# Attention and feed-forward on one core: exponents of the first block read from PSUM in pieces of 64 columns, one pair of banks for all quads, and a new order

## The chip, the cores and the metric

The kernel runs on one core of a Trainium2 chip. The metric is the device time of one execution in microseconds (us); less is better. TensorE multiplies, VectorE (DVE) and ScalarE (ACT) do the elementwise work, and SyncE (SP) issues the DMAs. Each engine works through its own queue in order; a queue's head that waits holds back all that stands behind it.

## What is computed

Chunked attention (32 queries against 8 memory keys, 16 keys to the left, the 32 of the chunk and 8 to the right, so 64 keys), then a feed-forward of two matrices with a squared, clipped activation between them:

```python
for c in range(24):                                   # chunks of 32 of a sequence of 768; batch 4, heads 8, head_dim 64
    scores = scale * q_c @ k_full.T                   # 32 x 64
    scores = scores - max(scores)                     # of each row
    a = exp(scores); a = a / (sum(a) + 1e-9)
    out[c] = a @ v_full
x = out as 3072 tokens x 512
h = x @ w_in                                          # 512 x 2048
g = where(h >= 1, h, where(h <= -1, 0, (h + 1)**2 / 4))
result = g @ w_out                                    # 2048 x 512, float32
```

## The kernel before

The tokens are cut into six blocks of 512. Blocks 0 and 1 go through the feed-forward with plain products, in steps of 128 columns of the hidden layer: `half_step` for half a block (A and B in the order), `step` for a whole one (E and F). Each float32 operand is split into a high and a low float32r part, and three products stand for one. Blocks 2 to 5 use a seven-product scheme: `product` makes the first layer by quads of four hidden slices (four quads per block), `unit` the second layer. The weights arrive by 16 loads of 1 MB as 64-bit words, which `decode` (w) turns into the two parts; `build` (t) and `build_out` (T) later make the sums that the seven products need.

`first_attention(g)` (g0 to g3) is the attention of block 0 in four units; units 0 and 1 are the first half of the block's tokens, 2 and 3 the second. For one unit: TensorE makes scores in PSUM (128 rows x 512 columns, that is 8 groups of 64), VectorE takes the maximum of each group (`mx`) and writes scores less maximum to SBUF (`pr`), ScalarE takes one exponent over the 512 columns, VectorE sums (`den`), adds 1e-9, inverts (`rin`) and multiplies; TensorE transposes `pr` into a bank, ScalarE copies it (`pt`), TensorE multiplies it with the values (`ps_x`), and ScalarE and VectorE split the result into `xth` and `xtl`. Units 2 and 3 keep their scores in the same pair of banks (`a1`, in `PLACES`). The loads of the four units' `first_qk` stand among the weights on the one DMA queue (`LOADS`). Nothing of the feed-forward can start before units 0 and 1 are through.

What stands where on each engine is written out by hand: `ORDER` is a table of some 1,860 names, each of which advances one piece of work by one step, and each engine keeps that order. `begin_second` (B in the table) takes the two `ps_h` banks for the quads as X and Y. In block 2, `bank_of` gives the second quad (n == 1) two other banks, `ps_g`, out of the four that the sums `ps_o` of blocks 0 and 1 have freed. A quad's result is read from X and Y by copies, relus and additions (`copy_out`, `relus`, `add_up`).

All instructions are issued through one helper, so every row names L150; rows are told apart by their tiles.

Of the kernel before, what the change touches and what calls it, by code (L numbers as in the profile page):

```python
# [9 lines left out]
F32 = mybir.dt.float32  # L10
# [18 lines left out]
    + + + + + g0 g0 g0 + g0 g1 + g1 g0 g0 g1 w0 g1 g0 g0 g1 g0 + + g1 g1 g1 w0 g2 g1 g0 g0 g1 g1 +  # L29
    g2 g2 w0 g2 g0 w0 g1 g2 g2 g3 + + g2 g2 w1 g2 + g0 g1 w0 + g3 g3 g3 w1 g3 g3 A0 g3 w2 g3 g2 A0  # L30
    g3 w1 A0 g2 w0 g3 w1 + g2 + w0 g3 g2 g3 + g3 A1 w3 w1 w1 B0 A2 + A1 w2 B0 w2 + w1 A0 A2 B0 A0
    B0 B1 A1 A0 w5 A2 w3 w3 B2 B0 w2 A1 A1 w4 w2 w3 w5 B1 B2 + + w3 B0 w4 w5 A1 + w6 B1 A3 A2 B3 B1
    A2 w4 A2 + n0 + B1 A3 A3 E4 B2 w5 w5 B2 B3 w4 B2 w7 B3 n0 A3 n0 w6 E4 w9 E6 w4 A3 n0 w8 E5 w7
    w6 B3 B3 E5 w7 w7 E4 B1 w6 w10 A3 E5 w7 w9 B3 E4 E8 E4 E5 E6 E5 w6 n0 w12 E4 B2 E6 + E8 w8 w9
    E6 w8 w9 + E7 w8 E6 E7 E5 w11 E8 E4 w9 E7 w11 w14 n0 w11 E6 E8 w8 w11 w11 E5 E8 w10 E7 E10 n0
    E9 E10 E7 w10 w10 w14 n0 E10 n0 w10 E8 E7 w14 + E9 E7 w12 E8 w14 E11 w13 w12 E9 n0 w12 E9 E10
    E10 E12 E9 E12 w15 w12 E9 n0 E6 n0 E11 w13 E12 E9 E11 n0 w14 w15 w13 n0 E11 E12 E13 E11 w13 w15
    E10 E13 w13 E13 n0 E12 n0 E14 n0 E12 E14 E11 n1 t1 n0 E10 t1 E14 C0 E12 n1 w15 E14 + E13 n1 E13
    E11 n1 n1 C0 n1 n1 n1 C1 + n1 E14 C1 n1 n1 w15 C2 E15 C0 n1 n1 E15 E13 E15 n1 E13 E15 n1 C0 t1
    E15 n1 n1 t1 n1 C2 C1 E15 E14 t1 D0 C2 E15 E14 C2 E15 C1 D0 E15 D1 C1 C0 C3 n2 E15 F4 E15 C0 D1  # L40
# [1112 lines left out]
```

## Time and profile before

| | |
|---|---|
| median of 3 runs | 576.08 us (574.78 to 576.36) |
| the profiled execution's own time | 575.56 us |
| its span, first to last instruction | 573.7 us |
| TensorE busy | 557.2 us (97%) |
| VectorE busy | 473.8 us (83%) |
| ScalarE busy | 368.0 us (64%) |
| mean granted TensorE clock | 0.988 of full speed |

The span is the time from the first to the last instruction; 1.9 us of the profiled execution lie outside it. Busy times are of instructions, which overlap a little at their ends on VectorE and ScalarE. A wait is named by what came last before it ended.

### The profile page before, as it was taken

Reading aid. Unit: us, or ns where it says so; the run is one execution under the profiler, and the core shown is the slowest. Engines: PE = TensorE matmul, PEld = TensorE weight load, DVE = VectorE, ACT = ScalarE, POOL = GpSimd, SP = SyncE. Lnnn points to the kernel's source line nnn. Section 1 sums busy time; section 2 is a strip of 40 time slices with the busy share of each in tenths; the row PEclk is TensorE's granted clock in tenths of the full one; section 3 lists DMA queues with packets and bytes.
Section 4 is the critical chain, followed back from the end, with each engine's and each line's share of the span. In section 5 each row is a group of like instructions: output and inputs, shape, how many; then the busy total and the mean of one; then the engine's idle time right before and its main releaser. Section 6 shows DMA issues by size and latency. Waiting matters only on the chain.

```text
span 573.7 us, 15814 instructions
## 1 busy us (share of the span) xinstructions
PE 557.2 (97%) x6648; PEld 516.1 (90%) x6648; DVE 473.8 (83%) x870; ACT 368.0 (64%) x677; POOL 0.7 (0%) x6
## 2 busy tenths in 40 slices
PE   5799999999999999999999999999999999999997
PEld 3798888888888889899999999999999999999997
DVE  5899996866998988999999769888867979566696
ACT  2699967564656684696766656756576576565642
POOL 0000000000000000000000000000000000000000
PEclk8699999999999999999999999999999999999999
DMA  8999600505798757789978979888869956789432
GB/s 348 422 422 418 282 0 2 184 7 198 272 359 324 270 197 251 266 271 354 327 267 273 322 229 349 289 309 286 269 203 316 328 197 209 238 238 309 153 111 92
DMA packets 40758, 145.72 MB, mean 254 GB/s; under 512 B 4208, under 2 KB 4464, under 8 KB 36080
## 3 DMA queue, kind: packets, MB, share of 16 engines
q1 hardware_dynamic: 40688, 144.72, 71.6%
q8 instruction: 52, 0.85, 0.6%
q14 instruction: 18, 0.15, 0.1%
HBM read 115.34 MB, written 29.36 MB: 252 GB/s over the span
## 4 chain that ended last, share of the span: by engine, by line
PE 88%; DMA 6%; DVE 3%; ACT 2%; issue 1%; DVEq 0%
PE ps_o L150 41%; PE ps_h L150 41%; PE ps_x L150 3%; DMA qk<-in_first_qk_dram 3%; PE ps_s L150 3%; DMA wr<-saved 2%; DMA out_dram<-ob 1%; DVE pr L150 1%; PE ps_g L150 1%; DVE feo L150 1%; ACT gw L150 0%; DVE ob L150 0%; ACT gt L150 0%; DVE wr L150 0%; DVE f L150 0%
## 5 line engine op out<-in xcount | busy, mean ns | idle before, releaser
L150 PE MATMUL ps_h<-s,wr 128*128 128x256 f32 x720 | 94.4, 282 | 0.3 <-DMA wr<-saved 0.2
L150 PEld LDWEIGHTS ps_h<-s,wr 128*128 128x128 f32 x720 | 89.1, 188 | 0.9 <-DVE gsb L150 0.4
L150 PE MATMUL ps_h<-xth,wr 128*128 128x512 f32 (+1 forms) x320 | 89.0, 354 | 0.2 <-ACT wr L150 0.2
L150 PE MATMUL ps_o<-wr,gh 128*128 128x512 f32 x256 | 80.6, 396 | 0.0
L150 PE MATMUL ps_h<-a,wr 128*128 128x256 f32 x540 | 70.9, 282 | 0.4 <-issue 0.3
L150 PEld LDWEIGHTS ps_h<-a,wr 128*128 128x128 f32 x540 | 67.4, 188 | 0.9 <-issue 0.4
L150 PEld LDWEIGHTS ps_h<-xth,wr 128*128 128x128 f32 x320 | 57.0, 190 | 9.4 <-ACT wr L150 0.3
L150 PEld LDWEIGHTS ps_o<-wr,gh 128*128 128x128 f32 x256 | 47.2, 188 | 10.4
L150 PE MATMUL ps_h<-xtl,wr 128*128 128x512 f32 (+1 forms) x160 | 54.4, 352 | 0.0
L150 PE MATMUL ps_o<-wr,gsd 128*128 128x256 f32 x384 | 53.8, 282 | 0.0
L150 PE MATMUL ps_o<-wr,gsc 128*128 128x256 f32 x384 | 52.8, 282 | 0.0
L150 PE MATMUL ps_o<-wr,gsb 128*128 128x256 f32 x320 | 50.8, 282 | 0.0
L150 PE MATMUL ps_o<-wr,gl 128*128 128x512 f32 x128 | 50.5, 394 | 0.0
L150 PEld LDWEIGHTS ps_o<-wr,gsd 128*128 128x128 f32 x384 | 49.0, 188 | 0.1
L150 PEld LDWEIGHTS ps_o<-wr,gsc 128*128 128x128 f32 x384 | 48.6, 188 | 0.2 <-DVE gsc L150 0.2
L150 ACT ACTIVATE gw<-ps_h 128x512 f32<-128x512 f32 (+1 forms) x55 | 29.6, 539 | 28.3 <-PE ps_h L150 19.8
L150 PEld LDWEIGHTS ps_o<-wr,gsb 128*128 128x128 f32 x320 | 43.9, 188 | 0.2
L150 ACT ACTIVATE gw<-gw 128x512 f32<-128x512 f32 (+1 forms) x72 | 42.6, 592 | 0.6
L150 ACT COPY gt<-ps_h 128x512 f32<-128x512 f32 x45 | 26.2, 583 | 16.7 <-PE ps_h L150 14.2
L150 PEld LDWEIGHTS ps_h<-xtl,wr 128*128 128x128 f32 x160 | 30.7, 192 | 4.3
L150 DVE TENSOR_TENSOR gt<-gt,ps_h 128x512 f32<-128x512 f32 x30 | 20.4, 680 | 12.0 <-ACT gt L150 5.9
L150 ACT COPY pt<-pr 32x512 f32<-32x512 f32 x40 | 24.7, 618 | 8.2 <-DVE pr L150 7.4
(106 smaller groups left out, 1012.0 us busy)
## 6 DMA issues: line engine op xcount, KB each, us to landing
wr<-saved SPq DMA_DIRECT2D x112, 512.0 KB, 4.9
w<-in_w_dram SPq DMA_DIRECT2D x16, 1024.0 KB, 18.6
qk<-in_qk_dram SPq DMA_DIRECT2D x10, 1536.0 KB, 7.1
v<-in_vw_dram SPq DMA_DIRECT2D x10, 1024.0 KB, 7.3
saved<-st SPq DMA_DIRECT2D x16, 512.0 KB, 4.0
plain_g<-gw SPq DMA_DIRECT2D x32, 256.0 KB, 4.7
gr<-plain_g SPq DMA_DIRECT2D x16, 512.0 KB, 4.4
saved<-wr SPq DMA_DIRECT2D x24, 256.0 KB, 4.0
```

The costliest lines, as they stand in the source:

```text
L150: return self.tc.keep_in_program_order(getattr(self.engine, name)(*args, **kwargs))
```

## The change

Three things change, and no arithmetic is left out.

1. In `first_attention`, for all four units (`BY_ROWS`), VectorE no longer writes scores less maximum and no longer sums. It multiplies the maxima by -scale (8 columns), and ScalarE takes the exponents straight from PSUM in eight activations of 64 columns, each with one column of `mx` as its bias and one column of `den` as its running sum.
2. `bank_of` loses its case for the second quad of block 2, which now uses X and Y like all others.
3. `ORDER` is written anew, with the same names but for one step less in each of g0 to g3. `LOADS`, and so the sequence on the DMA queue up to block 1, is the same.

```diff
 ORDER = """
-    + + + + + g0 g0 g0 + g0 g1 + g1 g0 g0 g1 w0 g1 g0 g0 g1 g0 + + g1 g1 g1 w0 g2 g1 g0 g0 g1 g1 +
...
-    def normalise(pr):
+    def normalise(pr, den=None):
         n = pr.shape[1]
-        den = apool.tile([P, n], F32, name="den", bufs=2)
-        dve.tensor_reduce(den, pr, axis=AX.X, op=ALU.add)
-        yield
+        if den is None:
+            den = apool.tile([P, n], F32, name="den", bufs=2)
+            dve.tensor_reduce(den, pr, axis=AX.X, op=ALU.add)
+            yield
         dve.tensor_scalar_add(den, den, 1e-9)
...
+    BY_ROWS = (0, 1, 2, 3)
...
-        p4 = pr.rearrange("p (h n) w -> p h n w", h=2)
-        dve.tensor_tensor(p4, s, m3.unsqueeze(3).to_broadcast([P, 2, n, W]), op=ALU.subtract)
-        yield
-        act.activation(pr, pr, AF.Exp, scale=SCALE)
-        yield
-        yield from normalise(pr)
+        if g in BY_ROWS:
+            dve.tensor_scalar(mx, mx, -SCALE, None, op0=ALU.mult)
+            yield
+            den = apool.tile([P, NG], F32, name="den", bufs=2)
+            for i in range(NG):
+                h, k = divmod(i, n)
+                act.activation(
+                    pr[:, i], s[:, h, k], AF.Exp, bias=mx[:, i : i + 1], scale=SCALE, accum_out=den[:, i : i + 1]
+                )
+            yield
+            yield from normalise(pr, den)
...
     def bank_of(name, key):
-        n = order[SECOND].index(key[1])
-        if key[0] == SECOND and n == 1:
-            if (n, name) not in bank:
-                for k in range(2):
-                    bank[n, "XY"[k]] = single(2 * n - 2 + k, "ps_g")
-            return bank[n, name]
         return bank[name]
```

**First place: the start of ScalarE's queue.** `pr_145` and `pr_138` hold units 0 and 1, `pr_324` and `pr_336` units 2 and 3; `w_105` and `w_176` are the first weights. Before:

```order
L150 ACT_TABLE_LOAD
L150 ACTIVATE pr_145<-pr_145 128x512 [waits DVE_49]
L150 ACTIVATE w_105<-w_105 128x1024 [waits DMAHW2_49]
L150 ACTIVATE pr_145<-pr_145 128x512 [waits DVE_49]
L150 COPY pt_146<-ps_h 128x512 [waits PE_49] x2
L150 ACTIVATE pr_324<-pr_324 128x512 [waits DVE_49]
```

After:

```order
L150 ACT_TABLE_LOAD [waits DVE_49]
L150 ACTIVATE pr_138,den<-ps_s,mx 128x64 [waits PE_49]
L150 ACTIVATE pr_138,den<-ps_s,mx 128x64 x7
L150 ACTIVATE w_176<-w_176 128x1024 [waits DMAHW2_49]
L150 ACTIVATE pr_138,den<-ps_s,mx 128x64 [waits DVE_49,PE_49]
L150 ACTIVATE pr_138,den<-ps_s,mx 128x64 x7
L150 CAST wr_258<-f 128x2x256 [waits DVE_49,Activation_49]
L150 COPY pt_139<-ps_h 128x512 [waits PE_49] x2
L150 CAST wr_258<-f 128x2x256
L150 ACTIVATE pr_336,den<-ps_s,mx 128x64 [waits DVE_49,Activation_49]
L150 ACTIVATE pr_336,den<-ps_s,mx 128x64 x7
L150 CAST xth<-ps_x 128x2x256 [waits PE_49]
```

Each exponent of 512 columns has become eight rows of 64. The load of the activation table stood free at the head of the queue; it now stands behind a wait for VectorE, whose first result for ScalarE is the scaled maximum of unit 0.

**Second place: VectorE's queue from the end of unit 2 to the end of unit 3.** Before, with `f` and `wr` the pieces of the weights' decoding:

```order
L150 TENSOR_TENSOR xtl<-ps_x,xth 128x2x256 [waits Activation_49] x2
L150 TENSOR_TENSOR wr_334<-f,wr_334 128x2x256
L150 TENSOR_REDUCE mx<-ps_s 128x8 [waits PE_49]
L150 TENSOR_TENSOR pr_324<-ps_s,mx 128x512 [waits DVE_49]
L150 TENSOR_SCALAR f<-w_206 128x1024 [waits DMAHW7_49,Activation_49]
L150 TENSOR_REDUCE den<-pr_324 128x8 [waits Activation_49]
L150 TENSOR_SCALAR den<-den 128x8 [waits DVE_49]
L150 RECIPROCAL rin<-den 128x8 [waits DVE_49]
L150 TENSOR_TENSOR pr_324<-pr_324,rin 128x512 [waits DVE_49]
L150 SCALAR_TENSOR_TENSOR f<-w_206,f 128x1024
```

After:

```order
L150 RECIPROCAL rin<-den 128x8 [waits DVE_49]
L150 TENSOR_TENSOR pr_336<-pr_336,rin 128x512 [waits DVE_49,PE_49]
L150 TENSOR_TENSOR wr_258<-f,wr_258 128x2x256
L150 TENSOR_TENSOR xtl<-ps_x,xth 128x2x256 [waits Activation_49]
L150 TENSOR_SCALAR f<-w_267 128x1024 [waits DMAHW7_49,Activation_49]
L150 TENSOR_REDUCE mx<-ps_s 128x8 [waits PE_49]
L150 TENSOR_SCALAR mx<-mx 128x8 [waits DVE_49]
L150 TENSOR_TENSOR xtl<-ps_x,xth 128x2x256 [waits Activation_49]
L150 SCALAR_TENSOR_TENSOR f<-w_267,f 128x1024
L150 TENSOR_SCALAR den<-den 128x8 [waits Activation_49]
L150 RECIPROCAL rin<-den 128x8 [waits DVE_49]
L150 TENSOR_TENSOR pr_336<-pr_336,rin 128x512 [waits DVE_49]
```

The two wide steps between a unit's maximum and its 1e-9 are gone; the 1e-9 of unit 2 (the row just ahead of the piece) and its multiplication, a low part of the weights, the first `xtl` and a shift of the second weights now stand ahead of the maximum of unit 3, and the other `xtl` and the second weights' long step between its scaled maximum and its 1e-9.

**Third place: ScalarE's queue at the second quad of block 2.** The copy of the quad's third sum is the row `gt<-ps_g` before, and the last row `gt<-ps_h` after. Before:

```order
L150 CAST wr_861<-feo 128x2x256
L150 CAST gsb<-gk 128x512
L150 CAST gsc<-gs 128x512
L150 COPY gt<-ps_g 128x512
L150 CAST wr_945<-feo 128x256
L150 COPY pt<-pr 32x512 x2
```

After:

```order
L150 CAST wr_786<-feo 128x256
L150 COPY ob<-ps_o 128x512
L150 COPY gt<-ps_h 128x512
L150 CAST gsb<-gk 128x512
L150 CAST wr_784<-feo 128x2x256
L150 COPY u_3055<-ps_h 128x512
L150 COPY gt<-ps_h 128x512
L150 CAST gsc<-gs 128x512
```

The cast of `gsc`, which takes a sum of VectorE's, stood ahead of that copy and now stands behind it.

On TensorE there, the third sum's product (`s_2648` before, `s_2680` after) and the next product on the same bank (`a_2651` before):

```order
L150 MATMUL ps_g<-s_2648,wr_1095 128x256 [waits DMAHW6_49,Activation_49]
L150 MATMUL ps_g<-s_2648,wr_1095 128x256 x11
L150 MATMUL ps_h<-a_2511,wr_962 128x256 [waits DMAHW7_49]
L150 MATMUL ps_h<-a_2511,wr_962 128x256 x11
L150 MATMUL ps_g<-a_2651,wr_1052 128x256 [waits DMAHW0_49,Activation_49]
L150 MATMUL ps_g<-a_2651,wr_1052 128x256 x11
L150 MATMUL ps_g<-s_2816,wr_1114 128x256 [waits DMAHW1_49,DVE_49]
```

After:

```order
L150 MATMUL ps_h<-s_2680,wr_1220 128x256 [waits DMAHW4_49,Activation_49]
L150 MATMUL ps_h<-s_2680,wr_1220 128x256 x11
L150 MATMUL ps_o<-wr_445,gsa 128x256 [waits PE_49]
L150 MATMUL ps_o<-wr_445,gsa 128x256
L150 MATMUL ps_o<-wr_445,gsa 128x256 [waits DVE_49]
L150 MATMUL ps_o<-wr_658,gsa 128x256 x3
L150 MATMUL ps_o<-wr_598,gsb 128x256 x2
L150 MATMUL ps_o<-wr_598,gsb 128x256 [waits DVE_49]
L150 MATMUL ps_o<-wr_740,gsb 128x256 x3
L150 MATMUL ps_o<-wr_258,gsb 128x256 [waits PE_49]
L150 MATMUL ps_o<-wr_258,gsb 128x256 x2
L150 MATMUL ps_o<-wr_598,gsb 128x256 x3
```

Before, one product of 12 matmuls for another quad stood between the two. Now 18 matmuls of the second layer (`ps_o`, of `gsa` and `gsb`) do; the next row after the piece is the quad's next product on that bank.

## Rows read from the trace of the kernel before

**Rows 1.** The page's head: span, and TensorE's busy time.

```profile
span 573.7 us, 15814 instructions
...
PE 557.2 (97%) x6648; PEld 516.1 (90%) x6648; DVE 473.8 (83%) x870; ACT 368.0 (64%) x677; POOL 0.7 (0%) x6
```

**Rows 2.** Stretches: length, busy us (and instructions) by engine, granted clock, DMA.

```profile
0.00:10.00 10.00, 5.05 (x136) 2.41 (x136) 3.81 (x9) 2.49 (x3) 0.70 (x6) 1.00 0.79 319
10.00:20.00 10.00, 6.88 (x200) 5.88 (x200) 8.93 (x18) 5.46 (x9) 0.00 (x0) 0.55 1.02 419
20.00:30.00 10.00, 8.33 (x222) 7.79 (x223) 7.42 (x13) 6.27 (x13) 0.00 (x0) 0.77 1.02 424
```

**Rows 3.** TensorE's waits in the whole span: us in total, times, longest.

```profile
PE ps_s L150 <- DMA qk<-in_first_qk_dram: 4.3, 4, 2.3
PE ps_h L150 <- DVE pr L150: 4.2, 2, 3.3
...
PE ps_g L150 <- ACT gt L150: 1.4, 1, 1.4
```

**Rows 4.** TensorE in order of time, units 0 to 3: start, us, operation, [idle before].

```profile
13.75 1.11 PE L150 MATMUL ps_h<-ident,pr 128*128 128x128 f32 x4
14.79 3.64 PE L150 MATMUL ps_x<-pt,v 64*64 64x32 f32 x128
...
20.72 1.29 PE L150 MATMUL ps_s<-qk 64*32 64x64 f32 x64 [2.29 <-DMA qk<-in_first_qk_dram]
...
26.18 0.63 PE L150 MATMUL ps_h<-ident,pr 128*128 128x128 f32 x4 [0.95 <-DVE pr L150]
26.73 2.07 PE L150 MATMUL ps_x<-pt,v 64*64 64x32 f32 x128
```

**Rows 5.** VectorE in order of time: the first maximum, then unit 3.

```profile
6.17 0.69 DVE L150 TENSOR_REDUCE mx<-ps_s 128x8 f32<-128x512 f32 x1
...
22.05 0.69 DVE L150 TENSOR_REDUCE mx<-ps_s 128x8 f32<-128x512 f32 x1 [1.64 <-PE ps_s L150]
...
24.17 0.69 DVE L150 TENSOR_REDUCE den<-pr 128x8 f32<-128x512 f32 x1
24.89 0.17 DVE L150 TENSOR_SCALAR den<-den 128x8 f32<-128x8 f32 x1
...
25.34 0.69 DVE L150 TENSOR_TENSOR pr<-pr,rin 128x512 f32<-128x512 f32 x1
25.95 1.22 DVE L150 SCALAR_TENSOR_TENSOR f<-w,f 128x1024 uint32<-128x1024 uint32 x1
```

**Rows 6.** ScalarE in order of time: its first row, then unit 3 and after.

```profile
0.73 1.28 ACT L150 ACT_TABLE_LOAD   x1 [0.73 <-PEq L1139]
...
23.50 0.64 ACT L150 ACTIVATE pr<-pr 128x512 f32<-128x512 f32 x1 [3.39 <-DVE pr L150]
24.05 1.14 ACT L150 ACTIVATE w<-w 128x1024 f32<-128x1024 f32 x1
25.09 0.56 ACT L150 COPY pt<-ps_h 128x512 f32<-128x512 f32 x1
25.55 0.38 ACT L150 ACTIVATE gw<-ps_h 128x256 f32<-128x256 f32 x1
25.83 0.38 ACT L150 ACTIVATE gt<-ps_h 128x256 f32<-128x256 f32 x1
```

**Rows 7.** ScalarE's activations out of PSUM by shape: busy us, mean ns.

```profile
L150 ACT ACTIVATE gw<-ps_h 128x512 f32<-128x512 f32 x39 | 23.4, 599 | 25.5 <-PE ps_h L150 17.0 <-DVE gl L150 6.1 <-DMA wr<-saved 2.3
...
L150 ACT ACTIVATE gw<-ps_h 128x256 f32<-128x256 f32 x16 | 6.3, 392 | 2.8 <-PE ps_h L150 2.7
```

**Rows 8.** TensorE in order of time at block 2's second quad.

```profile
244.54 1.69 PE L150 MATMUL ps_g<-a,wr 128*128 128x256 f32 x12 [1.41 <-ACT gt L150]
```

**Rows 9.** ScalarE there: the cast and the copy behind it.

```profile
243.24 0.62 ACT L150 CAST gsc<-gs 128x512 fp32r<-128x512 f32 x1 [0.92 <-DVE gs L150]
243.90 0.59 ACT L150 COPY gt<-ps_g 128x512 f32<-128x512 f32 x1
```

More of the change, by code (lines that the diff above doesn't have):

```diff
@@ new lines @@
+    F4 t4 F4 C1 t1 t4 + D2 F6 D3 t2 F5 F7 t4 t2 t4 F6 t2 t4 n2 t4 n2 n2 F6 n2 F6 F6 D2 t2 t2 F5 F5
+    t5 D2 F4 + F8 F5 n2 D2 t5 t5 D3 C3 F5 t2 n2 t5 n2 t5 t2 t2 t5 F5 F8 t5 t3 F8 t5 F8 t7 D3 n2 F9
+    D3 F5 t3 n2 D2 n2 t3 F7 t3 F8 D2 t7 t3 D1 t7 F9 n2 t7 t7 t3 F11 t7 t3 F9 D3 F7 F9 t7 F10 t3 F7
+    t6 t6 F9 F11 F8 t7 t6 t6 t6 F11 T0 n3 F7 F8 F12 n2 T0 F11 T0 T0 t6 T0 n3 T0 F10 F10 F9 F11 t6
+    n3 T0 n3 F10 F13 t6 n3 n3 T1 T1 T1 T1 F11 T1 F10 n3 n2 T0 T1 n3 n3 F10 F13 T0 T1 n3 T1 + n3 F13
@@ new lines @@
+    30c3 2u6r 2u4ld 2u4q3 4x 2u4q6 3kS4 30a22 3jS4 2u5s3 2u5s1 30m11 30p4 2u5s2 2u5s4 4x 30r22
+    2u5hc 2u4q7 30p3 30r21 2u5lc 2u4q5 31p1 30a12 2u5q7 2u5hd 2u5q5 2u5ld 2u5q6 2u5q3 4x 4x 2u6s3
+    30m21 31p2 2u6s1 2u6s2 2u6ha 2u6hb 4x 2u6s4 2u6la 4x 30r12 2u6hc 2u6lc 2u6q1 31c1 31p6 2u6lb
+    30m22 2u6q5 30m12 2u6q7 2u6q4 31c2 2u6q2 2u6hd 2u7r 4x 31p7 2u5ha 4x 2u6ld 31a11 2D8 31c3 4x
+    2u5la 4x 31r11 31p5 2u5hb 31a22 31p4 31p3 2u7s3 31a12 4x 4x 4x 2u6q3 31r12 2u6q6 31m11 2u7s1
+    2u7s2 31r21 2u5q1 4x 31m21 2u5lb 2u7ha 2u7la 4x 31r22 3u0s1 32p1 2u7s4 32c1 2u7hc 31m22 3u0s2
@@ new lines @@
+    2E8 3u2s2 4kA11 4y 33a22 3u2q4 3u2hc 3u2q2 3u0q1 3u2s4 4jA11 3u2hd 33m11 3u2ld 4y 33p3 33a12
+    33r12 3u2lc 33m12 4y 3u3hb 3u3s3 3u3s1 3u3s2 33r22 3u2q3 3u2q6 3u2q7 3u1ha 33m22 3u2q5 33p4
+    3u3ha 4y 3u3hc 3u3lb 4y 3u1la 3u3lc 4dS3 33r21 3u3la 4dS1 40p2 4kS3 3u3s4 3u1q1 3u3q7 3u3q5
+    4dS2 3u3hd 3u3q1 3u5s3 33m21 4kA22 40p1 3u3ld 3u5hb 3u3q2 4dS4 3u3q4 3u5s1 4kS2 4jS3 3u3q6 40c1
+    4jS2 40a11 3u3q3 3D0 40p6 4jA22 4kS1 4jS1 3u4r 3u5s2 3u5ha 3u5s4 40c2 3D1 3D2 4kS4 40p5 3D3 3D4
+    40r11 3u5lb 40p7 3D6 3u5hd 3u5q2 40m11 3u5la 3u5ld 3u5q4 3u5q1 4jS4 40c3 3u5hc 3u5lc 40a22
@@ new lines @@
+    3u4s3 3D5 3D7 3u6r 40p4 3u4s1 3D8 5x 5x 3u5q7 3u5q5 40r21 5x 40p3 3u5q3 5x 40a12 3u4s2 40m21
+    3u5q6 3u4s4 5x 3u4hb 41p2 3u4lb 3u6ha 5x 41p1 41c1 3u4q2 3u6s3 3u4hd 3u4q4 5x 41p6 40r12 3u6la
+    3u4ld 3u6q1 5x 40r22 3u4q6 3u4ha 41a11 3u4q3 40m12 3u4la 3u7r 5x 3u6s1 3u6hb 3u4hc 5x 41c2
+    41r11 41p5 3u4lc 3u6s2 3u6s4 41p7 41m11 41c3 3u4q5 3u4q7 3u6lb 3u4q1 3u6hd 40m22 41a22 3u6q4 5x
+    3u7s3 3u6q2 3u6ld 41p4 3u7s1 3u6hc 3u6lc 3u6q6 5x 4u0s3 3u6q3 3u7s2 41r21 3u6q7 3u6q5 3u7s4
+    3u7ha 3u7la 3u7hc 41p3 3u7q1 4u0s1 41r22 41a12 41m21 42p1 3u7lc 3u7hb 4u0s2 3u7q5 5x 3u7q7
@@ new lines @@
+    5dS4 4u5q7 4u5q5 5jS2 50r11 4u5hd 4u6r 5jS1 4u5q1 4u5ld 4u7r 5kS4 4u6s3 4u6s1 50p6 5jS3 4u5q3
+    50c2 50p5 4u5q6 4u6hc 50p7 50m11 4u6ha 50c3 5jA22 4u6lc 4u6q5 4u6s2 4u7s3 4u7s1 4u6q7 4u6s4
+    50p4 50a22 4u6hd 4u6hb 4u6ld 5jS4 50r21 50p3 4u6q6 4u6lb 4u7s2 4u6la 4u6q3 4u6q1 50a12 4u6q4
+    4u7ha 50r22 51p2 4u7s4 4u7la 4u7hc 50m22 50r12 51p1 51c1 4u6q2 4u7lc 4u7q1 51a11 51p6 4u7hb
+    51r11 51p5 51c2 51p7 50m21 4u7lb 4u7q2 50m12 4u7q7 51m11 51c3 4E0 4u7q4 51p4 51a22 4u7hd 51p3
+    5u0s3 5u0s1 51r21 4E1 4u7q5 4u7ld 5u1ha 4u7q6 51a12 5u1s3 51r22 52p1 5u0ha 4E2 51m21 52p2 52c1
@@ L121 @@
+    5u6q3 5u7q1 5u7lc 5u7hd 5u6q4 5E0 5u7lb 5u7q2 5u7ld 5u7q6 5u7q7 5E1 5Ea 5E2 5u7q5 5E3 5u7q4 5E4
+    5E6 5E7 5Eb 5u7q3 5E5 5E8
 """
@@ L369, in first_attention @@
         yield
-        p4 = pr.rearrange("p (h n) w -> p h n w", h=2)
-        dve.tensor_tensor(p4, s, m3.unsqueeze(3).to_broadcast([P, 2, n, W]), op=ALU.subtract)
-        yield
-        act.activation(pr, pr, AF.Exp, scale=SCALE)
-        yield
-        yield from normalise(pr)
+        if g in BY_ROWS:
[9 more added lines that the diff above has]
+            yield from normalise(pr, den)
+        else:
+            p4 = pr.rearrange("p (h n) w -> p h n w", h=2)
+            dve.tensor_tensor(p4, s, m3.unsqueeze(3).to_broadcast([P, 2, n, W]), op=ALU.subtract)
+            yield
+            act.activation(pr, pr, AF.Exp, scale=SCALE)
+            yield
+            yield from normalise(pr)
         ps = ps_h.tile([P, 512], F32, name="ps_h")
```

152 lines of the change are left out of this document (61 added, 91 removed).

## The prediction

> **What bounds the kernel now.** I read the page's head first: TensorE is busy for 557.2 of 573.7 us [rows 1]. So an edit counts only through TensorE's 16.5 idle us and through its slow stretches. Next come the stretches of 10 us: in the first three TensorE is idle for 4.95 + 3.12 + 1.67 = 9.7 us, and its granted clock is 0.55 and 0.77 in the second and third, a mix of the levels 1.2 and 2.4 GHz [rows 2]. The waits name the causes: the loads of `first_qk` 4.3 us, VectorE's `pr` 4.2, and, as the longest that is not of the start, one wait of 1.4 for a copy of ScalarE [rows 3].
>
> The timelines then say which wait of the start ends last. Unit 3's scores wait for their load until 20.72 [rows 4]. The load queue is unchanged and moves 419 and 424 GB/s there [rows 2], so no edit brings that start forward, and what units 0 to 2 do sooner is worth nothing. From it a chain runs without a gap: scores, maximum at 22.05, exponent at 23.50, sum at 24.17, 1e-9 at 24.89, multiplication 25.34 to 26.03 [rows 5, 6]; only then do unit 3's transposes start, 26.18, after 0.95 idle [rows 4]. That is the last idle of the start: 0.72 before 20.72 and 0.95 are the third stretch's 1.67 [rows 2]. Hence two places are worth working out: the time of unit 3's transposes, and the 1.41 at 244.54.
>
> **The eight activations: their price.** No row of before has an activation with a column of memory as bias or with a running sum. Nearest are activations out of PSUM: 599 ns for 512 columns and 392 for 256 [rows 7], so 0.81 ns per column and, for 64, 392 - 192 x 0.81 = 237 ns. Two in a row start 0.28 apart at 256 columns (25.55, 25.83) [rows 6], so 0.28 - 0.155 = 0.125 at 64. Lower end: 0.125 each, if bias and sum cost nothing. Upper end: the whole 0.237 without overlap plus 0.17, what the smallest step of VectorE takes to write 8 columns [rows 5]: 0.41. I take 0.30: the sum of each has to be complete before the next begins one, so I count no overlap (0.24), and a third of the small write for bias and sum. Eight are 2.4 us (1.0 and 3.3 at the ends). The one exponent that goes took 0.64 [rows 6].
>
> A price that only a page states: the Trainium skill, "ScalarE: Activation LUTs", section "What ACT_TABLE_LOAD costs", gives an activation with such a bias some 280 ns + 0.83 per column and an overlap of some 93 ns; that would be an estimate of 0.24 each, nothing said of the sum, and by the walk below unit 3 would then come 0.6 us later than before. No run here has shown it yet.
>
> **The start, walked with 2.4 us per unit.** The order shows the table load (1.28) behind a wait for the first scaled maximum. It stood free at 0.73 [rows 6]; now it begins when that maximum is there, 6.17 + 0.69 + 0.2 = 7.1 [rows 5], and ends at 8.4. ScalarE then does unit 0 to 10.8, the first weights (1.05 net of overlap) to 11.9, unit 1 to 14.3. VectorE's 1e-9, multiplication of unit 0, inversion and multiplication of unit 1 stand behind that sum: 0.2 + 0.7 + 0.25 + 0.7, to 16.2, with unit 0 ready at 15.3. TensorE's transposes take 1.1 per unit at the low clock and the values 3.64 for both [rows 4]: transposes to 17.6, values to 21.2. ScalarE copies unit 1 to 18.2 and casts weights to 18.8, and has unit 2 ready at 21.2. Its scores' banks are those of unit 3, so unit 3's scores start at 21.2 instead of 20.72 and end at 22.5 (1.29) [rows 4].
>
> VectorE is now late: from 21.2 it has unit 2's 1e-9 and inversion (0.45), the multiplication (0.65) and three steps of 0.6 (a low part, an `xtl`, a shift) before the maximum of unit 3, which starts at 24.15 instead of 22.05. Maximum 0.7, scaling 0.2, eight activations 2.4: 27.5. VectorE's `xtl` and its 1.22 us step are over by then. From 1e-9 to the end of the multiplication it took 24.89 to 26.03 = 1.15 [rows 5]: 28.65, and the transposes start at 28.8 instead of 26.18. **Term: +2.6 us.** The matmuls of the first half step that stand ahead of them are done by 27.2 even at the low clock, so nothing covers it.
>
> The same walk at the ends: with 1.0 per unit, units 0 to 2 are early, the maximum stands at 22.05 as before, and the exponents end at 24.0; but the 1.22 us step now precedes the 1e-9 and ends at 24.8, so the transposes start at 26.1: -0.1. What the removed steps of 0.69 free on VectorE is hidden by the load and by that step. With 3.3 per unit, ScalarE's serial work pushes each unit in turn (values to 22.9, unit 2's exponents to 23.7, unit 3's to 30.9): 32.1, or +5.9. The table load itself is covered up to some 1.4 per unit and is in the walk beyond.
>
> **The bank case and the order at block 2.** Before, the second quad's fourth product on X waited 1.41 us [rows 8] for the copy at 243.90, and that copy stood on ScalarE behind the cast of `gsc`, which itself waited 0.92 for VectorE [rows 9]. Now the cast stands behind the copy, and TensorE has 18 matmuls between the product and its successor, 18 x 0.12 = 2.1 us (12 start in some 1.5 us at full clock [rows 8]) against 0.6 for the copy. **Term: -1.4 us.** What is late next there is VectorE's parts for these 18 matmuls; bounds: -1.7, if the other idle of that stretch goes too, to 0, if they are as late as `gsc` was. With one pair of banks the second quad's first product has to wait for the last reads of the first quad's: a relu and a copy of 0.6 each on ScalarE; 6 matmuls of 512 columns (1.4 us) stand between. I take nothing, at most 1.1.
>
> **The rest of the new order** carries the same steps, and TensorE's matmuls are as many, so their time is the same at the same clock. VectorE loses eight steps of 0.69 and gains four of 0.2, all in the first 30 us, where it waits anyway. I count zero, with one more us of waits as the bound on the bad side.
>
> **Sum.** 573.7 + 2.6 - 1.4 = 574.9 us of span. The profiled execution had 575.56 - 573.7 = 1.9 outside its span, so 576.8, against a median of 576.08 (the profiled execution lies 0.5 under it and within the runs). 0.3% is 1.73 us, about what a measurement of this kernel tells from no change: "same" is 574.35 to 577.8.
>
> **The rivals.**
> *Dear activations (slower).* Place: ScalarE's queue from 8.4 to unit 3. If bias and sum each cost what a separate small step does, eight take 2.9 and more: at 2.9, between the walks of 2.4 and 3.3, the start is 2.6 + 0.5/0.9 x 3.3 = +4.4, so 575.6 + 4.4 - 1.4 = 578.6. It decides from 2.7 per unit on. For it: two extras that no row prices, and each delay is met again by the next unit. Against: activations without these extras overlap by 0.1 of their 0.38 [rows 6].
>
> *The clock (slower).* The granted clock is low for much of 10 to 30 [rows 2]. If the gaps ahead of unit 3's multiplication keep it low past the transposes, the values take 3.64 instead of 2.07 [rows 4]: +1.6, 578.4. Against: it had risen by 26.73, when the values took 2.07, while TensorE worked on after 20.72 [rows 4]; TensorE works there now too, though with gaps.
>
> *Cheap activations (faster).* With 1.0 to 1.6 per unit the start is -0.1 to +0.3 and the 1.4 remains: 575.6 - 0.1 - 1.7 = 573.8 to 574.4. For it: the spacing of 0.125. It decides below 1.6, which is 0.20 per activation.
>
> *The order gains elsewhere (faster).* After the first 30 us TensorE idles for 16.5 - 9.7 = 6.8 us, the end of the kernel included [rows 1, 2]; if the new order removes 3 of them and the start costs 1, 573.6. Nothing in the rows asks for it.
>
> That the change doesn't do what it says is out: the eight rows per unit stand in the order.
>
> **How the numbers follow.** Forecast (1.6 to 2.7 per unit, the wait of 1.4 gone): 0.45, no change that can be told. Dear activations 0.25, clock or the new hand-over of banks 0.08: slower 0.33. Cheap 0.16, order elsewhere 0.06: faster 0.22. The likeliest case's own range is 574.4 to 577.8. The range for 8 in 10 goes from the cheap case, 573.7, to the upper end of the walk without the bounds on the bad side, 575.6 + 5.9 - 1.4 = 580.1.
>
> **What would show it.** Right: the table load near 7.1 us; eight rows of `pr,den` spaced by about 0.3; unit 3's maximum after 23.5 and its transposes near 28.8; no wait for a copy of ScalarE at the second quad. Wrong: a spacing under 0.2 or over 0.34; transposes of unit 3 before 27 (then faster) or after 30 (slower); new waits of TensorE over 1 us between 90 and 570; or a clock still at the lower level after 29.

## The result, and the profile after

The changed kernel took 582.59 us, median of six runs (577.79 to 584.75), the kernel before 576.15 beside it: ratio 1.0107, 95% interval 1.0085 to 1.0129. It is slower by 1.1%, and the time lies above the range of the prediction (580.1). The profiled execution of the changed kernel is the shortest of its six; the other five have a mean granted clock of 0.975 to 0.979 against its 0.985. So its trace shows the change at its best, and what the other five lose on top had to be found with further kernels.

The page's head of the changed kernel (span; TensorE's busy time):

```profile
span 576.0 us, 15866 instructions
...
PE 558.3 (97%) x6648; PEld 516.7 (90%) x6648; DVE 468.7 (81%) x866; ACT 376.0 (65%) x737; POOL 0.7 (0%) x6
```

TensorE's waits over its whole span (total, times, longest; `issue` is a wait for which the profile names no cause):

```profile
PE ps_s L150 <- DMA qk<-in_first_qk_dram: 6.7, 3, 5.1
PE ps_s L150 <- issue: 1.4, 1, 1.4
PE ps_h L150 <- DVE pr L150: 1.2, 1, 1.2
...
PE ps_h L150 <- DMA wr<-saved: 0.7, 1, 0.7
PE ps_h L150 <- ACT gt L150: 0.5, 1, 0.5
PE ps_o L150 <- DVE gsd L150: 0.5, 1, 0.5
PE ps_o L150 <- DVE gsa L150: 0.3, 1, 0.3
```

The 1.4 on `gt` that [rows 3, 8] show is gone. Small ones of 0.3 to 0.7 stand in the list after the start; the kernel before has others there, of 0.2 to 0.6. ScalarE and VectorE at the start of the same trace:

```profile
7.21 1.28 ACT L150 ACT_TABLE_LOAD   x1 [7.21 <-DVE mx L150]
8.51 0.32 ACT L150 ACTIVATE pr<-ps_s,mx 128x64 f32<-128x64 f32 x1
8.72 0.19 ACT L150 ACTIVATION_READ_ACCUMULATOR pr<-ps_s,mx 128x1 f32 x1
8.81 0.31 ACT L150 ACTIVATE pr<-ps_s,mx 128x64 f32<-128x64 f32 x1
...
10.84 1.14 ACT L150 ACTIVATE w<-w 128x1024 f32<-128x1024 f32 x1
```

```profile
23.98 0.69 DVE L150 TENSOR_REDUCE mx<-ps_s 128x8 f32<-128x512 f32 x1 [0.19 <-PE ps_s L150]
...
27.48 0.17 DVE L150 TENSOR_SCALAR den<-den 128x8 f32<-128x8 f32 x1 [0.88 <-ACT pr L150]
27.69 0.20 DVE L150 RECIPROCAL rin<-den 128x8 f32<-128x8 f32 x1
27.93 0.69 DVE L150 TENSOR_TENSOR pr<-pr,rin 128x512 f32<-128x512 f32 x1
```

One activation starts 0.30 us after the other (8.51, 8.81), as two rows: 0.32 for the exponents and 0.2 for reading out the sum, partly over each other; eight are 2.33 us (8.51 to 10.84). TensorE, which answers to [rows 4]:

```profile
12.96 1.18 PE L150 MATMUL ps_s<-qk 64*32 64x64 f32 x64 [5.07 <-DMA qk<-in_first_qk_dram]
15.29 1.94 PE L150 MATMUL ps_h<-ident,pr 128*128 128x128 f32 x8 [1.14 <-DVE rin L150]
17.16 3.64 PE L150 MATMUL ps_x<-pt,v 64*64 64x32 f32 x128
21.00 0.45 PE L150 MATMUL ps_s<-qk 64*32 64x64 f32 x13 [0.21 <-DVE den L150]
22.88 1.06 PE L150 MATMUL ps_s<-qk 64*32 64x64 f32 x51 [1.42 <-issue]
...
28.77 0.63 PE L150 MATMUL ps_h<-ident,pr 128*128 128x128 f32 x4 [1.22 <-DVE pr L150]
29.32 2.07 PE L150 MATMUL ps_x<-pt,v 64*64 64x32 f32 x128
```

Unit 3's transposes start at 28.77 instead of 26.18, the walk's 28.8. The stretches of 10 us, as [rows 2], now with the fourth:

```profile
10.00:20.00 10.00, 5.90 (x180) 5.24 (x182) 5.01 (x11) 8.17 (x41) 0.00 (x0) 0.55 1.02 422
20.00:30.00 10.00, 7.15 (x162) 6.20 (x159) 7.60 (x15) 7.75 (x30) 0.00 (x0) 0.60 1.02 418
30.00:40.00 10.00, 10.00 (x163) 9.70 (x156) 8.14 (x14) 9.90 (x25) 0.00 (x0) 1.00 1.02 425
```

In the third stretch TensorE is 1.2 us less busy than before and its granted clock is 0.60 instead of 0.77, but from 30 us on it is 1.00. Against the 573.7 of [rows 1] that execution lost 2.3 us of span; the others, with spans of 579.6 to 583.0, lost 6 to 9.

### The profile page after: what moved, and what is told of

Its sections match the earlier page's. It is cut to its first block, busy times and chain, and to the rows that moved or that the text cites. A ratio compares the mean times of both kernels' runs of the same rounds, so it can differ in the third digit from the quotient of the medians.

```text
span 576.0 us, 15866 instructions
## 1 busy us (share of the span) xinstructions
PE 558.3 (97%) x6648; PEld 516.7 (90%) x6648; DVE 468.7 (81%) x866; ACT 376.0 (65%) x737; POOL 0.7 (0%) x6
## 4 chain that ended last, share of the span: by engine, by line
PE 92%; ACT 3%; DMA 2%; DVE 1%; issue 1%; DVEq 0%; ACTq 0%
PE ps_h L150 43%; PE ps_o L150 43%; PE ps_x L150 4%; PE ps_s L150 3%; ACT pr L150 2%; DMA wr<-saved 1%; DMA qk<-in_first_qk_dram 1%; ACT pt L150 0%; DVE mx L150 0%; DVE ob L150 0%; DVE pr L150 0%; ACT L150 0%; ACT gk L150 0%; ACT gt L150 0%; ACT w L150 0%
## 5 line engine op out<-in xcount | busy, mean ns | idle before, releaser
L150 PE MATMUL ps_h<-s,wr 128*128 128x256 f32 x768 | 99.5, 282 | 0.5 <-ACT gt L150 0.5
L150 PEld LDWEIGHTS ps_h<-s,wr 128*128 128x128 f32 x768 | 94.8, 188 | 1.2 <-ACT gt L150 0.7
L150 PE MATMUL ps_h<-a,wr 128*128 128x256 f32 x576 | 76.2, 282 | 0.7 <-DMA wr<-saved 0.7
L150 PEld LDWEIGHTS ps_h<-a,wr 128*128 128x128 f32 x576 | 71.9, 188 | 1.7 <-ACT gsb L150 0.9
L150 ACT ACTIVATE gw<-ps_h 128x512 f32<-128x512 f32 (+1 forms) x56 | 30.1, 538 | 34.6 <-PE ps_h L150 28.9
L150 ACT COPY gt<-ps_h 128x512 f32<-128x512 f32 x48 | 28.0, 584 | 27.3 <-PE ps_h L150 25.7
L150 DVE TENSOR_TENSOR gt<-gt,ps_h 128x512 f32<-128x512 f32 x32 | 21.9, 683 | 13.0 <-PE ps_h L150 7.0
L150 ACT CAST gsd<-gs 128x512 fp32r<-128x512 f32 x32 | 19.8, 619 | 17.2 <-PE ps_o L150 16.3
```

The lines of the kernel that those rows point to most:

```text
L150: return self.tc.keep_in_program_order(getattr(self.engine, name)(*args, **kwargs))
```

## The experiments

Ratios and differences are against the kernel before measured beside each set of runs (576.4, 576.8, 576.6 and 576.8 us). Executions of one kernel spread by 2 to 7 us, so the times are judged by medians; a trace tells where its own execution spent its time.

**First: the change again, its two halves, and a filled gap.** The theory was the clock, the rival new waits. *again* is the changed kernel unaltered.

> The changed kernel once more, for its spread and a second trace. Its six executions ran from 577.8 to 584.8 us while the granted clock ran from 0.985 to 0.975, and the one trace at hand is the fastest. Theory A (the clock): in most executions TensorE's clock stays at its lower level some 10 us longer than in that trace (0.009 of mean clock is 0.018 x 580 = 10 us at half speed, 5.2 us lost); a trace of a 582 us execution then shows the same starts up to about 28 us and the lower level to 35 or later, or a second fall. Theory B (waits): the 5 us are new waits of TensorE on loads or on the other engines after the first 30 us, and the clock differs only as a consequence; the trace then shows 4 us or more of waits of TensorE after 30 us than the 2.6 there are in the first trace.

580.44 us (ratio 1.0066, 1.0044 to 1.0088). In its trace TensorE waits no more after 40 us than in the first; the clock is low from 8.4 to 28.9 us, and the transposes come at 29.66. *fill* adds three dummy matmuls ahead of unit 3's transposes:

```diff
         ps = ps_h.tile([P, 512], F32, name="ps_h")
+        for _ in range(3 if g == 3 else 0):
+            pe.matmul(ps, warm[:, 0:P], warm, start=True, stop=True)
```

> The changed kernel with three more matmuls of 512 columns, on data that nobody reads, ahead of the transposes of unit 3, where TensorE waits 1.2 us for VectorE. They write the bank that the transposes then overwrite. Theory A (the clock): TensorE has no gap before those transposes, so the clock rises by 28 to 29 us in all executions: 577 to 579 us, clock 0.984 or more. Theory B (waits): nothing changes, 581 to 584 us with a clock of 0.976, or 0.5 us worse for the extra matmuls.

578.45 us (1.0036, 1.0017 to 1.0054): 2 us below *again* although it adds work. Ten of its twelve executions have a mean clock of 0.982 to 0.985 (the other two 0.997 and 1.000); of the twelve of the changed kernel, the six above and those of *again*, ten have 0.975 to 0.982, one 0.985 and one 0.996. *neworder_oldexp* keeps the new order and the one pair of banks and takes the exponents as before; *oldorder_newexp* is the reverse.

```diff
...
-    BY_ROWS = (0, 1, 2, 3)
+    BY_ROWS = ()
```

> The new order and the one pair of banks, but the exponents of block 0 as before (subtraction, one exponent of 512 columns, sum), with the sum's step put back right behind each unit's exponent. If the loss is the eight activations (walk: +2.6 us of start, and with it the clock), this has unit 3's transposes near 26 us, a clock of 0.987 or more, no wait of 1.4 us at block 2's second quad, and 573.5 to 575.5 us. If the loss is in the new order, it stays at 579 us or more.

> The old order and the old banks, with the eight activations per unit (the sum's step taken out of each unit). If the eight activations are the loss, unit 3's transposes come 2 to 4 us later than 26.2, the wait of 1.4 us at block 2's second quad stays, and the time is 578 to 584 us, with a clock under 0.987. If the loss is in the new order, 576 us as before.

581.87 (1.0088) and 582.4 us (1.0088). The first was a miss: each half alone is as slow as both. VectorE's rows in *neworder_oldexp* say why it is:

```profile
26.09 0.69 DVE L149 TENSOR_REDUCE den<-pr 128x8 f32<-128x512 f32 x1 [0.69 <-ACT pr L149]
26.70 0.68 DVE L149 TENSOR_TENSOR xtl<-ps_x,xth 128x512 fp32r<-128x512 f32 x1
27.29 1.22 DVE L149 SCALAR_TENSOR_TENSOR f<-w,f 128x1024 uint32<-128x1024 uint32 x1
28.43 0.16 DVE L149 TENSOR_SCALAR den<-den 128x8 f32<-128x8 f32 x1
```

The new order sets an `xtl` and the 1.22 us step between sum and 1e-9; it is made for exponents whose sum comes from ScalarE. So unit 3's transposes came at 29.70 there, and its granted clock, back at 1.00 by 26, was 0.50 again from 29.3 to 39.6. In *oldorder_newexp* they came at 28.75. All the slow kernels had one thing in common: unit 3 late.

**Second: unit 3 late, nothing else.** *before_late* is the kernel before with four sums more for unit 3, whose result nothing reads:

```diff
         dve.tensor_reduce(den, pr, axis=AX.X, op=ALU.add)
+        if late:
+            for _ in range(4):
+                spare = apool.tile([P, n], F32, name="spare", bufs=2)
+                dve.tensor_reduce(spare, pr, axis=AX.X, op=ALU.add)
...
-        yield from normalise(pr)
+        yield from normalise(pr, g == 3)
```

> The kernel before, with nothing of the change, but four extra sums of unit 3's exponents (4 x 0.61 us of VectorE, into a tile that nothing reads) ahead of its 1e-9 addition, so that unit 3's transposes start at about 28.7 us instead of 26.18, where the changed kernel had them (28.77). Late-start theory (what costs is that unit 3's turn comes late, whatever makes it late: the delay itself and what TensorE's granted clock then does): 579 to 582 us, and TensorE idle 25.2 to 28.7 us. Theory that the loss lies in the new instructions or the new order: 577 to 578.7, the plain delay at most.

577.12 us (0.9992, 0.9969 to 1.0016): no loss, against the late-start theory, although its unit 3's transposes came at 28.64 and its clock stayed low to 37. At the matmuls that the kernel before reaches at 38.8 us its trace was 6.2 us behind, at the last copy 1.9: TensorE had caught up by small amounts all along. The new tile had moved all buffers behind it by 64 bytes. *before_shift* has that tile and not the sums; *before_late2* has the sums and not the tile, by `name="mx"` in place of `name="spare"`. The tile of *before_shift*:

```diff
+    calls = []
...
+        calls.append(n)
+        if len(calls) == 4:
+            pool.memset(apool.tile([P, 16], F32, name="spare", bufs=1), 0.0)
```

> The kernel before with nothing but a tile of 64 bytes per partition that nothing reads, placed as the extra sums' tile was in the run before_late: it moves the buffers behind it in SBUF (gt, gw, gsa to gsd, gh and the input's of block 1) by 64 bytes and changes no instruction but one memset on GpSimd. In the trace of before_late unit 3 came 2.5 us late and TensorE's clock stayed low to 37 us, so that it was 6.2 us behind the kernel before at 32 us, and yet only 1.9 us behind at the end; its 128x256 matmuls took 280 ns there and not 282. Address theory (the shift makes the matmuls 1% faster): 572 to 574.5. Otherwise: 576 to 577.

> The run before_late again without the shift: the four extra sums of unit 3 are written into a buffer that is there anyway, so that all tiles lie as in the kernel before. Late-start theory with the address theory: 579 to 582, as the changed kernel. If a late unit 3 truly costs nothing: 576.5 to 578.

571.34 us (0.992, 0.9897 to 0.9944) and 583.02 (1.0113, 1.009 to 1.0136). Two results. A late unit 3 costs 6.4 us without any part of the change. And 64 bytes are worth 5.3 us, which had hidden this. *after_shift* and *hot_shift* are the changed kernel and *hot* (below) with that tile:

> The changed kernel with the same 64 bytes. Address theory: 576 to 579, some 3 us below the changed kernel. Otherwise: 580 to 582.5.

> The run hot (dummy matmuls in the gaps) with the same 64 bytes. Address theory: 574 to 576.5, below the kernel before. Otherwise: 578 to 579.5, as hot.

576.54 (0.9997, 0.9975 to 1.0019) and 573.53 (0.9959, 0.9939 to 0.9979): the 64 bytes give some 5 us there too, so they change nothing in the comparison of the change.

**Third: the clock or the delay.** *before_late2* in the fourth stretch, and TensorE's rows around unit 3:

```profile
20.00:30.00 10.00, 5.79 (x96) 5.15 (x97) 8.26 (x16) 4.19 (x9) 0.00 (x0) 0.67 1.02 421
30.00:40.00 10.00, 10.00 (x164) 9.94 (x161) 5.23 (x9) 5.82 (x13) 0.00 (x0) 0.57 1.02 425
```

```profile
24.86 0.71 PE L150 MATMUL ps_h<-xth,wr 128*128 128x256 f32 x4
28.71 1.09 PE L150 MATMUL ps_h<-ident,pr 128*128 128x128 f32 x4 [3.14 <-DVE pr L150]
29.72 3.64 PE L150 MATMUL ps_x<-pt,v 64*64 64x32 f32 x128
...
37.30 0.42 PE L150 MATMUL ps_h<-xth,wr 128*128 128x256 f32 x1
...
38.87 0.28 PE L150 MATMUL ps_h<-xth,wr 128*128 128x256 f32 x1
```

The clock had risen by 25 us; TensorE stood still for 3.14, and then transposes, values and all matmuls to 38.7 us ran at the lower level, 1.2 GHz (granted clock 0.50 from 28.4 to 38.7; 0.42 for a matmul of 256 columns, 0.28 after). *late2_fill* puts eight dummies in that gap, with the delay kept:

> The run before_late2 (the kernel before with unit 3 made 2.4 us late, 583.02) with eight dummy matmuls (512 columns, bf16) ahead of unit 3's transposes, in the gap of 25.6 to 28.7 us in which TensorE stood still there and after which its granted clock fell a second time (0.50 from 28.3 to about 38 us). Clock theory: the clock stays at 1.00 after 25 us, the second low stretch and its 4.5 us go, and the time is 578 to 580. If the clock were only a companion: 582 to 584.

579.89 us (1.0065, 1.0043 to 1.0086).

```profile
25.63 1.89 PE L150 MATMUL ps_h<-warm 128*128 128x512 bf16 x8 [0.67 <-ACT pt L150]
28.26 0.66 PE L150 MATMUL ps_h<-ident,pr 128*128 128x128 f32 x4 [0.74 <-DVE pr L150]
28.85 2.07 PE L150 MATMUL ps_x<-pt,v 64*64 64x32 f32 x128
```

The values take 2.07 and not 3.64, and the loss falls from 6.4 to 3.1. (The durations tell the level here: this trace has no record of the lower one at the start, and a mean clock of 1.000, although the values of units 0 and 1 took 3.64. So a mean of 0.99 to 1.000 in an execution is no sign that the clock stayed up.) The copies of block 0's and the last block's output on ScalarE, of the kernel before, *before_late2* and *late2_fill* in turn, show that what is lost at the start stays lost:

```profile
132.39 0.59 ACT L150 COPY ob<-ps_o 128x512 f32<-128x512 f32 x1 [2.87 <-DVE ob L150]
...
565.87 0.37 ACT L150 COPY ob<-ps_o 128x256 f32<-128x256 f32 x1 [1.59 <-PE ps_o L150]
```

```profile
139.36 0.59 ACT L150 COPY ob<-ps_o 128x512 f32<-128x512 f32 x1 [2.86 <-DVE ob L150]
...
573.81 0.37 ACT L150 COPY ob<-ps_o 128x256 f32<-128x256 f32 x1 [1.59 <-PE ps_o L150]
```

```profile
134.62 0.59 ACT L150 COPY ob<-ps_o 128x512 f32<-128x512 f32 x1 [2.86 <-DVE ob L150]
...
569.14 0.38 ACT L150 COPY ob<-ps_o 128x256 f32<-128x256 f32 x1 [1.61 <-PE ps_o L150]
```

At 132 us they are 7.0 and 2.2 behind, at the end 7.9 and 3.3. So of the 7.0 some 4.7 went with the dummies (0.4 of it by scores that came a little earlier in that execution).

The changed kernel under the same test is *hot*: 14 dummies ahead of unit 2's scores, 4 ahead of the transposes of units 0 and 1, 4 ahead of unit 3's. *early_table* moves its table load to the start, by one activation of one element there; *early_hot* is both.

```diff
+        if g == 2:
+            keep_warm(14)
         src = qk_of[0, g].rearrange("p (r n) -> p r n", r=2)
...
+        if g == 0:
+            keep_warm(4)
         ps = ps_h.tile([P, 512], F32, name="ps_h")
+        for _ in range(4 if g == 3 else 0):
+            pe.matmul(ps, warm[:, 0:P], warm, start=True, stop=True)
```

> The changed kernel with dummy matmuls (512 columns, bf16) in TensorE's gaps of the start: 14 ahead of unit 2's scores, 4 ahead of the transposes of units 0 and 1, 4 ahead of unit 3's transposes. Clock theory: the granted clock stays at 1.00 through the start or falls for a few us only, TensorE's 10 to 11 us of work between 12 and 30 us shrink, and the time is 575 to 577.5, with little spread. If the clock has no part in it: 580 to 582 as the changed kernel.

> The changed kernel with one more activation of one element by the exponential ahead of everything on ScalarE, so that the table load (1.28 us at 7.21) lies at the start and not behind the first maximum. By the walk unit 0's eight activations start at 7.2 instead of 8.51, unit 1's end near 13 instead of 14.14, the transposes of units 0 and 1 start near 14 instead of 15.29, and unit 3's scores come 1.3 us earlier; unit 3's transposes at 27.5 instead of 28.77 if the scores follow. Late-start theory: 577 to 579. If scores of unit 3 are held by something else (its load, or the 1.4 to 2.5 us that TensorE stood among those scores for no cause that the profile shows): no gain, 580 to 582.

> Both edits together: the early table load and the dummy matmuls in the gaps. If the changed kernel loses by its late unit 3 and by the clock, and gains 1.4 us by the wait that it takes away at block 2, this one beats the kernel before: 573.5 to 576. If the loss lies elsewhere: 579 to 582.

*hot* took 579.06 us (1.0034, 1.0016 to 1.0051), *early_table* 580.17 (1.0059, 1.0039 to 1.0079), *early_hot* 578.36 (1.0033, 1.0015 to 1.0051). *hot* misses its numbers, since the gaps only closed in part: in its trace the clock still was 0.50 from 16.7 to 27 us and unit 3's transposes came at 30.31, 1.5 later than in the change. The early table load brought the transposes of units 0 and 1 forward to 14.30, but unit 3's scores still began at 20.82 with their load and stood 1.16 us (last section); unit 3's transposes came at 28.32, 0.45 earlier and not 1.3. The new one-element tile of *early_table* and *early_hot* also moves `gt`, `gh`, `gsa` to `gsc`, a part of `gsd`, the first values and the input of block 1 by 32 bytes. That wasn't tried by itself, so these two times are no clean measure of the table load.

**Last: the bytes, and the clock where unit 3 isn't late.** *before_shift128* is *before_shift* with 128 bytes. *before_hot_shift* adds to *before_shift* 11 dummies ahead of unit 0's transposes, 7 ahead of unit 3's scores and 2 ahead of its transposes.

> The run before_shift with 128 bytes instead of 64. If any move helps, or the buffers' distance to the ones that stay counts: 570 to 573.5. If it is the place modulo 128: 576 to 577, as the kernel before; then the change's own move of f, gs and rin by 128 bytes is no part of its loss either.

> The run before_shift with dummy matmuls in the gaps of the start: 11 ahead of unit 0's transposes, 7 ahead of unit 3's scores, 2 ahead of unit 3's transposes. In before_shift the granted clock was 0.50 from about 8.7 to 25.2 us, but unit 3's scores wait for their data and its transposes for VectorE, so that a faster clock there mostly makes these waits longer. Clock theory: 569.5 to 571.5, 0 to 1.5 us below before_shift. If the dummies delay real work: 572 to 573.

577.14 us (1.001, 0.9989 to 1.0032): not any move helps, and the place modulo 128 fits all three times. The change moves `f`, `gs` and `rin` by multiples of 128 bytes, and *oldorder_newexp*, which moves no buffer, loses as much; so this is no part of its loss. *before_hot_shift*: 573.17 us (0.9941), 1.8 above *before_shift*: in its trace unit 3's scores came only at 23.94 us, behind five of the seven dummies and a stop of TensorE of 4.41 among them (last section), and the higher clock didn't pay for it.

*before_shift* at 571.34 us is thus the fastest, below both kernels.

## Why the prediction was wrong

**The price of the activations was right, with some luck.** 0.29 to 0.30 each and 2.33 for eight, against 0.30 and 2.4. The prediction had 0.24 without overlap and a third of a small write; the trace has 0.2 from the start of the exponents to a row that reads out the sum, and 0.1 from there to the next. The Trainium skill, "ScalarE: Activation LUTs", section "What ACT_TABLE_LOAD costs", led to an estimate of 0.24; the trace has 0.05 more.

**The walk of the start was right in its sum:** table load 7.21 (7.1), unit 3's maximum 23.98 (24.15), exponents to 27.45 (27.5), transposes 28.77 (28.8): +2.59 of +2.6. That it fits so closely is partly luck. Unit 3's scores began at 21.00 (21.2), but most of them came at 22.88, after a stop of 1.42 that the walk doesn't have, and VectorE, late as walked, was ready 0.19 before them. Where the stop ends later, so do the transposes: 22.88 and 28.77 in this trace, 23.79 and 29.66 in that of *again*, 23.89 and 29.77 in that of *after_shift*, 22.44 and 28.32 in that of *early_table*, 5.87 to 5.89 us apart in all four.

**The wait at block 2 went,** as argued; nothing in the row of [rows 8] takes its place, and the nearest thing to a price of the bank hand-over is a wait of 0.5 on `gt`, in the list above. No time shows what that is worth: *again* is 2.0 below *oldorder_newexp*, which keeps that wait (1.6 in its trace) and the late unit 3, but the two intervals overlap, and the changed kernel's first six runs (582.59) are as slow as *oldorder_newexp* (582.4). From 40 to 570 us, in the kernel before and in the changed one (length, TensorE's busy time):

```profile
40.00:570.00 530.00, 526.76 (x6024) 490.76 (x6022) 443.10 (x817) 343.98 (x634) 0.00 (x0) 1.00 0.71 244
```

```profile
40.00:570.00 530.00, 527.70 (x6017) 490.84 (x6016) 443.68 (x816) 347.36 (x637) 0.00 (x0) 1.00 0.70 244
```

TensorE is idle for 3.24 and for 2.30 us there: of the 1.4 some 0.9 remains, the rest went into the other small waits, within the one us that the prediction gave as their bound. But the 0.9 doesn't reach the end. TensorE's last matmuls, before and after:

```profile
569.30 0.87 PE L150 MATMUL ps_o<-wr,gsd 128*128 128x256 f32 x6
```

```profile
571.65 0.87 PE L150 MATMUL ps_o<-wr,gsd 128*128 128x256 f32 x6
```

They start 2.35 later, of the 2.59 at unit 3's transposes. The rest went into TensorE's own time for the same matmuls: from the 601st to the last (dummies left out) it is busy for 529.9 us in the kernel before and 530.7 in the changed one. Ten traces with the buffers at the same places modulo 128 bytes range from 529.9 to 531.5, so 0.7 is within their spread.

**The step that failed is the clock rival: its price and its chance.** The sum has no term for the clock. The prediction let a late clock cost only the values, 3.64 instead of 2.07, +1.6, and put it with the bank hand-over at 0.08, because the clock had risen by 26.73 while TensorE worked on after 20.72. A clock that is low past the transposes is what happened; the price and the chance were wrong. When unit 3 is late, TensorE runs out of work at 25 to 27.5 us and stands still ahead of the transposes; the clock, whether it had risen or not, is then often at the lower level up to 37 to 40 us (to 36.9 in the trace of *after_shift*, 37.2 *before_late*, 38.7 *before_late2*, 39.6 *neworder_oldexp*), and every matmul until there takes longer, not the values alone. In *before_late2* and *late2_fill* this is 3.3 us of the loss by the medians (2.8 by the ratios), 4.7 between the two traces. The case of the changed kernel that shows it is the trace of *after_shift*, mean clock 0.975:

```profile
20.00:30.00 10.00, 6.58 (x129) 5.77 (x125) 6.90 (x14) 7.16 (x30) 0.00 (x0) 0.50 1.01 414
30.00:40.00 10.00, 10.00 (x169) 9.60 (x169) 4.95 (x9) 6.95 (x17) 0.00 (x0) 0.65 1.03 427
```

The granted clock there is low through unit 3 and to 37 us, which is the prediction's own sign of being wrong, "a clock still at the lower level after 29". The twelve executions of that one kernel show what it costs: five with a mean clock of 0.981 to 0.984 took 573.5 to 574.5 us, two with 0.975 and 0.976 took 579.0 and 579.2, and the other five lie between. The first trace of the change had the clock back at 28 us and lost little. By mean clock the five longer executions of the changed kernel belong with *after_shift*: 0.008 x 576 us is 4.6 us of lost clock, and they are 3.5 to 7 us longer. None of those five has a trace, so for them this rests on the mean clock and on *fill*, *late2_fill* and *after_shift*.

**The sum then reads:** late unit 3 +2.6 to +3.5 (28.77 in the first trace, 29.66 in that of *again*); next to nothing net after it (the last matmuls are 2.35 later in the first trace, 3.76 in that of *again*); and, in the executions without a trace, 3.5 to 7 us more than in the first trace, and 0.7 to 2.5 more than in that of *again*, which is the clock as far as the mean clock tells. That makes the medians of 582.6 and 580.4. The clock, at a chance of 0.08 together with another case, should have been the main one: the prediction had read that the low stretch ended in unbroken work after 20.72, and its own walk leaves TensorE without work from 27.2 to 28.8, ahead of the transposes.

## What to carry to other kernels

An edit that delays one step of a chain by 2.6 us can cost more than twice that (6.4 in *before_late2*) where the delay opens a gap on TensorE: price the work behind the gap at the lower clock level, all of it, and not only the next group. When a kernel with one tile more behaves against every theory, compare the buffers' addresses before thinking further: *before_late* would have cleared the late unit 3 wrongly. Half of a change under another half's order is no clean test: *neworder_oldexp* was slow for a reason of its own.

## What the runs showed of the hardware

**64 bytes, 5 us.** With all buffers behind `apool` moved by 64 bytes TensorE's matmuls are a little quicker in several groups. From the 601st matmul to the last, in the kernel before, *before_shift* and *before_shift128* (stretch, length, TensorE's busy time first):

```profile
36.71:569.89 533.18, 529.94 (x6041) 493.49 (x6040) 446.28 (x820) 347.27 (x640) 0.00 (x0) 1.00 0.71 246
```

```profile
36.77:567.68 530.91, 526.27 (x6041) 490.11 (x6040) 445.64 (x820) 346.78 (x640) 0.00 (x0) 1.00 0.71 247
```

```profile
36.88:571.61 534.73, 530.64 (x6041) 495.95 (x6040) 446.16 (x820) 346.93 (x640) 0.00 (x0) 1.00 0.71 245
```

The five traces with the 64 bytes have 524.8 to 526.3 us, the ten at the old places modulo 128 have 529.9 to 531.5, and the two with 32 bytes (*early_table*, *early_hot*) 531.9 and 531.7. The profiled *before_shift* is the longest of its six executions: around 402 us TensorE waits 1.6 us for `gsa`, and then its granted clock is 0.50 from 404.3 to 407.7, so that 2.6 us of lead over the kernel before turn into 0.8 behind. This is the fall of the clock behind a gap once more, in the middle of the kernel; behind the gap of 1.41 at 243 us in the kernel before there was none. Which of the moved buffers makes the matmuls quicker, and why, is open.

**A stop of TensorE that no semaphore ends.** In eleven traces (the changed kernel and all made from it, both halves and *before_hot_shift*) TensorE stops for 1.16 to 4.41 us just ahead of the 350th matmul of its queue, dummies counted: after the thirteenth of unit 3's scores, or, with dummies ahead, among the values or the dummies. The waits call it `issue`. The record of the DMA queues does show something: in all eleven the second packet of 16 KB on the queue that the page calls `q8 instruction` lands 1.27 to 1.50 us before TensorE goes on (21.38 and 22.88 in the change). In the six traces without the stop the same packet lands 2.25 to 2.51 us before the 350th matmul (18.50 and 20.95 in the kernel before). And the twelve other waits of over 0.25 us that are called `issue`, from 0.3 to 1.95 us, end 1.28 to 1.58 us after such a packet too. So TensorE most likely waits there for its own instructions; no run moved a packet, and why it comes late is open. In the changed kernel this stop is a part of what makes unit 3 late, as the four traces above show, and why an early table load gained only 0.45.

**A sum costs a row.** Each activation with a running sum is followed by a read-out of 0.19 to 0.29 us, of which 0.1 to 0.2 lies beside the next activation.
